# Block-diagonal products moved from GpSimd to VectorE, two small outputs kept as columns, and a new order, in a decode step with its gradients

## The chip, the cores and the metric

One core of a Trainium2 chip runs the kernel. The metric is the device time of one execution in microseconds (us). Before the change the median of seven runs is 478.31 us (475.49 to 484.51).

## The reference

The forward function adds three terms, for a batch of 2 with one position and width D = 576:

```python
xn = _layernorm(x)
out = x + A(xn, k_cache, v_cache, wq, wo) + B(xn, w_gate, w_up, w_down)
# A: q = xn @ wq, 32 heads of 128 on 16 key/value heads, 4096 cached positions
#    p = softmax(q k^T / sqrt(128)); o = p v; o @ wo
# B: (xn @ w_gate * (xn @ w_up)) @ w_down, inner width 4608
```

The kernel returns `out` (out_0) and the gradients for `grad_out` with respect to x (out_1), k_cache and v_cache (out_2, out_3, 2 x 16 x 4096 x 128 each), wq, wo, w_gate, w_up and w_down (out_4 to out_8), all bf16. For each cached head the gradient is a product of a column over positions and a row over the 128 channels: for v it is p times the row of the gradient arriving at o, for k it is the gradient of the scores times q. Two query heads share one cached head, so each such gradient is a sum of two.

## The kernel before, in words

All of k_cache and v_cache is read once (64 tiles of 1 MB) and gradients of the same size are written (64 stores of 1 MB); the weights and their gradients are the rest. Sixteen SBUF buffers of 1 MB, the tiles "big", serve as loaded caches (kv), transposed tiles (X) and outgoing results (st).

Attention goes in 16 steps: step s has a group g of two cached heads (4 query heads) and one batch row b, and in each step k (t = 0) and v (t = 1) are handled for both heads l. Of a step:

- `load_kv` loads the four tiles over SP's DMA queue.
- `turn` transposes each tile in 32x32 blocks on VectorE (L421), in two halves, into an X tile.
- `build_W` copies the query (or the arriving gradient) on GpSimd (POOL) into a stationary operand (L1071).
- `softmax` and `dscore` multiply X by it on TensorE (PE, L1106) and go through chains of small steps that pass between PE, VectorE (DVE) and ScalarE (ACT): L1172 to L1199 and L1227 to L1238. They end in transposed weights pp and dd.
- `build_BD` makes the block-diagonal operand of the outer products. A row of 128 channels per partition (vr) is multiplied by a mask of 16 columns (mask16), so that a tile BD of 128 x 16 x 128 has the row in one block and zeros in the others: L1094, one instruction on POOL for each of 32 cases (16 steps, two for each). There are three BD tiles and two vr tiles.
- `head_outer` multiplies pp or dd by BD on PE (L1128), four units of [128, 2, 512] for each cached head. Each is copied from PSUM into an st tile by ACT (L425) or DVE (L427), and the finished tile goes out on SP (L652).
- `contract` multiplies the weights by the loaded tile (L1283) and folds the result (L1300) into oT; only then is the loaded tile free.

Around these steps run `group_front` and `group_back` (projections with wq and wo and their gradients) and `mlp`, nine slices of the second branch. Their outgoing tiles leave over POOL's DMA queue (L652 as well), and most weights come in over it (L1010 to L1032).

The order is written out while the program is built. Each part is a generator that yields what it needs next: an engine and an estimated cost, a buffer, an event or a DMA. A planner (`Order`) runs these against a clock of its own. It takes the request that can start first; among requests on the same engine within SLACK of that one it takes the lowest priority. `pr(name, s)` is 28 s + PR[name], with HEAD and TAIL added in the first two and the last two steps. An eviction (`EV`) goes to ACT or DVE, whichever would end first. CAP limits how many of the 16 big buffers each use may hold, and LM is a margin that is added to a planned landing. The result is one fixed, in-order list of instructions for each engine and DMA queue. An instruction that waits holds everything behind it on the same engine.

Two small results are summed over the whole kernel. `acc` (128 partitions x 5 x 2, fp32) collects out_0 as columns, and `accx` (128 x 160) collects the gradient of xn. At the end, `final_out` adds x to acc and brings the columns into two rows of 576: L1332 multiplies the saved rows `xy` by an identity, L1346 and L1349 multiply acc by an fp32 identity, L1326 (ACT) and L1327 (DVE) copy the rows, and L1328 stores them on SP. `final_dx` folds accx (L1366, L1368), forms the gradient through the layer norm with DVE steps (L1372 to L1383) and a product with a mean column (L1377), and brings the columns into rows through L1332, L1387 and L1390. At the start, `front` computes the layer norm and also turns x into columns (xnT, L599 to L611).

Of the kernel before, what the change touches and what calls it, by code (L numbers as in the profile page):

```python
# [9 lines left out]
ALU = mybir.AluOpType  # L10
# [3 lines left out]
P = 128  # L14
# [229 lines left out]
def PE(stream, issue=0.0, quad=None, kind="f"):  # L244
    return ("op", "PE", max(CLK * stream, issue) + 0.03, quad, stream, issue, kind)


def DVE(cost):
    return ("op", "DVE", cost)
# [38 lines left out]
def DMA(engine, cost, nbytes, row=8192):  # L288
# [3 lines left out]


NBIG, NGU, NWW, NBD = 16, 1, 5, 3
CAP = {"kv": 8, "X": 8, "st": 12}
MLP0, MLPD = 0, 7.51
KVSTORE = "SP"
WQ0, WO0 = 0, 1
LATENCY, DRY = {"SP": 0.5, "ACT": 0.5, "POOL": 0.57}, 0.4
LM = 0.0  # L300
CLK = 2.0
BIAS = 0.47
SLACK = {"PE": 0.07, "ACT": 0.08, "DVE": 0.41, "POOL": 10.49, "SP": 43.83}
STEP = 28.0
HEAD = {"turn0": 6.6, "att": -11.1, "dsc": 103.3, "con": 16.6, "conv": -58.3, "out1": 57.1, "out0": -106.0, "front": 0.1, "back": -143.5, "W0": 3.2, "W1": 21.7, "BD1": -106.8, "BD0": -0.2, "load": 33.1}
TAIL = {"turn0": 19.4, "turn1": -1.3, "att": 13.2, "dsc": -10.2, "con": -0.3, "conv": -0.3, "out0": 63.9, "front": -9.4, "W0": 5.3, "W1": 19.3, "BD0": -29.4, "load": -20.4}
PR = {"turn0": 125.0, "turn1": -93.7, "att": -589.3, "dsc": -604.4, "conv": 187.4, "con": -216.4, "out1": 1081.4, "out0": 424.1,
      "front": 268.7, "back": 51.9, "W0": 161.4, "W1": 725.8, "BD1": 945.4, "BD0": -58.5, "mlp": -97.3, "wout": -241.3,
      "store": 861.0, "load": 135.3, "wload": -180.4, "fin": 113.9, "const": 215.4, "mload": 362.2}


def pr(name, s):
# [5 lines left out]
def kernel(  # L318
# [128 lines left out]
    meanc = filled("meanc", [P, 1], FP32, 1.0 / D)  # L447
    xnT = filled("xnT", [P, 12], FP32, 0.0)
    nrT = const.tile([P, 4], FP32, name="nrT")
    gg = const.tile([P, 2, 12], FP32, name="gg")  # L450
    gp4 = const.tile([P, 4], FP32, name="gp4")
    zero1 = filled("zero1", [P, 1], FP32, 0.0)
    acc = filled("acc", [P, 5, 2], FP32, 0.0)
# [69 lines left out]
    def carve(t, n):  # L523
        return pairs(t[:])[0:2, D * n:D * (n + 1)]

    xy = const.tile([2, 2 * D], BF16, name="xy")

    def front():
        xb, yb = xy[:, 0:D], xy[:, D:2 * D]
        for t, src in ((xb, A_x), (yb, grad_out)):  # L530
            yield DMA("ACT", 0.45, 2304, 1152)
            nc.scalar.dma_start(t, src.rearrange("b s d -> (b s) d"))
# [55 lines left out]
        yield WAIT(Econst)  # L588
        nr = gg[0:2, 0, 0:4]
        yield DVE(0.3)  # L590
        nc.vector.memset(gg[:, 1], 0.0)
        nc.vector.tensor_scalar(nr[:, 0:2], identf[0:2, 0:2], nmu[:], None, op0=ALU.mult)
        nc.vector.tensor_scalar(nr[:, 2:4], identf[0:2, 0:2], rstd[:], None, op0=ALU.mult)
        i = yield ACQ("m")
        tp, bp = m_t[i], m_t[i][:, 64:68]
        yield PE(0.0, 0.3)
        for a in range(4):
            for c in range(4):
                nc.tensor.matmul(tp[32 * c:32 * c + 32, 2 * a:2 * a + 2], lhsT=xb[:, P * c + 32 * a:P * c + 32 * a + 32],  # L599
                                 rhs=ident[0:2, 0:2], start=True, stop=True)  # L600
        for a in range(2):
            nc.tensor.matmul(tp[0:32, 8 + 2 * a:10 + 2 * a], lhsT=xb[:, 512 + 32 * a:544 + 32 * a],
                             rhs=ident[0:2, 0:2], start=True, stop=True)
        nc.tensor.matmul(bp, lhsT=view(ones[:], 0, 2, 0, [[0, P]]), rhs=nr, start=True, stop=True)
        yield DVE(0.9)
        nc.vector.tensor_copy(xnT[:, 0:8], tp[:, 0:8])
        nc.vector.tensor_copy(xnT[0:32, 8:12], tp[0:32, 8:12])
        nc.vector.tensor_copy(nrT[:], bp)
        for k, op in ((0, ALU.add), (2, ALU.mult)):
            nc.vector.tensor_tensor(xnT[:], xnT[:], view(nrT[:], 0, P, k, [[0, 6], [1, 2]]), op)  # L610
# [465 lines left out]
    def build_BD():  # L1076
        for s in range(NS):
            g, b = divmod(s, Bq)
            for t in (1, 0):
                yield PRIO(pr(f"BD{t}", s))  # L1080
                yield WAIT(Econst)
                yield WAIT(grp[g]["Eq"], grp[g]["Ed"])
                v = yield ACQ("vr")
                m = yield ACQ("m")
                yield PE(0.053)
                nc.tensor.matmul(m_t[m][:, 0:P],
                                 lhsT=qr_t[grp[g]["qs"]][:, t, b, :],
                                 rhs=ident[:], start=True, stop=True)
                e = yield EV(128)
                cp(e, vr_t[v][:], m_t[m][:, 0:P])  # L1090
                yield REL("m", m)
                i = yield ACQ("BD")
                yield POOL(3.6)
                nc.gpsimd.tensor_tensor(BD_t[i][:], view(vr_t[v][:], 0, P, 0, [[0, 16], [1, Dh]]),  # L1094
                                        view(mask16[:], 0, P, 0, [[1, 16], [0, Dh]]), ALU.mult)
                yield REL("vr", v)
                bS[s][t] = i
                yield SET(bE[s][t])
# [223 lines left out]
            yield PRIO(pr("front", 2 * g))  # L1322
            yield from group_front(g)

    def rows_put(o, n, out):
        nc.scalar.copy(view(xy[:], 0, 2, n * D, [[P, 5], [1, 64]]), o[0:2, 0, 0:320].rearrange("p (k n) -> p k n", k=5))  # L1326
        nc.vector.tensor_copy(view(xy[:], 0, 2, n * D + 64, [[P, 4], [1, 64]]), o[0:2, 1, 0:256].rearrange("p (k n) -> p k n", k=4))  # L1327
        nc.sync.dma_start(out.rearrange("b s d -> (b s) d"), xy[:, n * D:(n + 1) * D])  # L1328

    def rows_add(o, n):  # L1330
        for k in range(2):
            nc.tensor.matmul(o[0:2, k, 0:320 - 64 * k], lhsT=ident[0:2, 0:2],  # L1332
                             rhs=view(xy[:], 0, 2, n * D + 64 * k, [[P, 5 - k], [1, 64]]), start=True, stop=False)

    def final_out():
        yield PRIO(PR["fin"])
        yield WAIT(Eprep, *acc_E)
        i = yield ACQ("o")
        o = o_t[i]
        yield PE(1.1, 0.5)  # L1340
        rows_add(o, 0)
        for dc in range(5):
            r = slice(0, P) if dc < 4 else slice(64, P)
            for k in range(2):
                if dc < 4:
                    nc.tensor.matmul(o[0:2, k, 64 * dc:64 * dc + 64], lhsT=acc[:, dc, :],  # L1346
                                     rhs=identf[:, 64 * k:64 * k + 64], start=False, stop=(dc == 3 and k == 1))
            if dc == 4:
                nc.tensor.matmul(o[0:2, 0, 256:320], lhsT=acc[64:P, 4, :], rhs=identf[64:P, 64:P],  # L1349
                                 start=False, stop=True)  # L1350
        yield ACT(0.4)
        yield DVE(0.4)
        yield DMA("SP", 0.3, 2304, 1152)
        rows_put(o, 0, out_0)
        yield REL("o", i)

    def final_dx():
        yield PRIO(PR["fin"])
        yield WAIT(Eprep, *accx_E)
        i = yield ACQ("o")  # L1360
        o = o_t[i]
        m = yield ACQ("m")
        mt = m_t[m]
        g, gx = gg[:, 0], gg[:, 1]
        yield PE(0.3, 0.3)
        nc.tensor.matmul(mt[:, 0:8], lhsT=accx[:, 0:P], rhs=F8[:], start=True, stop=True)  # L1366
        for k in range(2):
            nc.tensor.matmul(mt[0:32, 8:12], lhsT=accx[:, P:160], rhs=F8[:, 4 * k:4 * k + 4],  # L1368
                             start=(k == 0), stop=(k == 1))
        rows_add(o, 1)  # L1370
        yield DVE(0.5)
        nc.vector.tensor_copy(g[:, 0:8], mt[:, 0:8])  # L1372
        nc.vector.tensor_copy(g[0:32, 8:12], mt[0:32, 8:12])
        nc.vector.tensor_tensor(gx, g, xnT[:], ALU.mult)
        nc.vector.reduce_sum(gp4[:], view(gg[:], 0, P, 0, [[12, 2], [1, 2], [2, 6]]), axis=AX.X)
        yield PE(0.0, 0.1)
        nc.tensor.matmul(mt[:, 16:20], lhsT=view(meanc[:], 0, P, 0, [[0, P]]), rhs=gp4[:], start=True, stop=True)  # L1377
        yield DVE(0.5)
        mean = [view(mt[:], 0, P, 16 + 2 * k, [[0, 6], [1, 2]]) for k in range(2)]
        nc.vector.tensor_tensor(gx, xnT[:], mean[1], ALU.mult)  # L1380
        nc.vector.tensor_tensor(gx, g, gx, ALU.subtract)  # L1381
        nc.vector.tensor_tensor(gx, gx, mean[0], ALU.subtract)  # L1382
        nc.vector.tensor_tensor(gx, gx, view(nrT[:], 0, P, 2, [[0, 6], [1, 2]]), ALU.mult)  # L1383
        yield REL("m", m)
        yield PE(0.4, 0.3)
        for a in range(4):
            nc.tensor.matmul(view(o[:], 0, 2, 512 * (a // 2) + 32 * (a % 2), [[64, 4], [1, 32]]),  # L1387
                             lhsT=gx[:, 2 * a:2 * a + 2], rhs=identf[:], start=False, stop=(a == 3))
        for a in range(2):
            nc.tensor.matmul(o[0:2, 0, 256 + 32 * a:288 + 32 * a], lhsT=gx[0:32, 8 + 2 * a:10 + 2 * a],  # L1390
                             rhs=identf[0:32, 0:32], start=False, stop=(a == 1))
        yield ACT(0.4)
        yield DVE(0.4)
        yield DMA("SP", 0.3, 2304, 1152)
        rows_put(o, 1, out_1)
        yield REL("o", i)

    od.spawn(front(), -1000.0)
    od.spawn(final_out(), PR["fin"])
# [42 lines left out]
```

## Time and profile before

| | before |
|---|---|
| median of 7 runs | 478.31 us |
| profiled execution, its own time | 479.3 us |
| its span, first to last instruction | 477.5 us |
| bytes moved | 185.93 MB, mean 389 GB/s |
| ACT evictions of 128x1024 (L425) | 267, mean 1027 ns |
| DVE evictions of 128x1024 (L427) | 41, mean 1212 ns |
| DVE transposes of 128x1024 (L421) of loaded tiles | 128, mean 1217 ns |
| granted TensorE clock, mean | 0.676 |

Engine rows of the profile give the line, the engine, the operation, what is written and read, the count, the busy time and the mean of one; behind the last bar stands the idle time of the engine in front of these instructions, and which instruction ended it. In a timeline the first two figures are the start in us from the span's start and the length. The page cuts the span into 40 slices of some 12 us: a digit is the busy share of a slice in tenths. The DMA share of a window is the mean busy share of the 16 DMA engines; it can read slightly over 1. A DMA engine counts as busy while a packet is under way, so the bytes per second stand beside it.

### The profile page before, as it was taken

How to read it: one execution, taken by the hardware profiler on the slowest of the kernel's cores; microseconds unless marked ns; L12 is line 12 of the kernel's file. 1: busy time of each engine (PE TensorE's matmuls, PEld its weight loads, DVE VectorE, ACT ScalarE, POOL GpSimd, SP SyncE). 2: the span in 40 equal slices, each digit the busy share in tenths (PEclk: the TensorE clock that was granted, in tenths of full speed). 3: DMA queues.
4: the chain of work that ended last, by engine and by line, in shares of the span. 5: the costliest groups of instructions: out<-in, count | busy, mean ns of one | idle time of the engine just before them, and what ended most of it. 6: DMA issues, size and time to landing. Idle time of an engine off the chain costs nothing. (4 is left out here: it accounts for less than half of the span.)

```text
span 477.5 us, 14608 instructions
## 1 busy us (share of the span) xinstructions
PE 374.6 (78%) x6122; PEld 212.2 (44%) x6122; DVE 349.9 (73%) x660; ACT 345.5 (72%) x527; POOL 244.8 (51%) x348
## 2 busy tenths in 40 slices
PE   0589978897869678785987899784989599779886
PEld 0446444444534345433453545433545254424543
DVE  7788777868659567785789856694576799678872
ACT  6069876775886667756787888771878577979984
POOL 6185716647379315593617384673434772664211
PEclk9998685757765666656597855556566675855885
DMA  8999999999999999999999999999999999999985
GB/s 304 386 405 372 410 388 414 406 400 401 419 412 363 390 424 345 379 417 402 419 371 419 410 418 408 402 425 404 410 328 408 421 404 385 405 405 426 360 318 191
DMA packets 33444, 185.93 MB, mean 389 GB/s; under 512 B 5034, under 2 KB 5170, under 8 KB 16994
## 3 DMA queue, kind: packets, MB, share of 16 engines
q1 hardware_dynamic: 19866, 139.61, 72.5%
q0 software_dynamic: 13504, 45.38, 25.3%
q8 instruction: 48, 0.79, 0.6%
q14 instruction: 18, 0.15, 0.1%
q10 hardware_dynamic: 8, 0.00, 0.0%
HBM read 92.48 MB, written 92.48 MB: 387 GB/s over the span
## 5 line engine op out<-in xcount | busy, mean ns | idle before, releaser
L425 ACT CAST big<-ps_o 128x1024 bf16<-128x1024 f32 (+1 forms) x324 | 288.3, 959 | 42.2 <-PE ps_o L1128 27.0
L421 DVE STREAM_TRANSPOSE big<-big 128x1024 f32<-128x1024 f32 x128 | 152.8, 1217 | 11.5 <-issue 4.7
L1094 POOL TENSOR_TENSOR BD<-vr,mask 128x2048 bf16<-128x2048 bf16 x32 | 115.2, 3602 | 43.8 <-ACT vr L425 25.9
L1106 PE MATMUL ps_m<-big,W 128*32 128x128 bf16 x2048 | 61.1, 286 | 10.1 <-DVE big L421 4.4
L427 DVE CAST big<-ps_o 128x1024 bf16<-128x1024 f32 (+1 forms) x52 | 57.8, 1115 | 9.1 <-ACT big L425 4.8
L1106 PEld LDWEIGHTS <-W 128*32 128x32 bf16 x2048 | 48.4, 127 | 29.3 <-issue 28.1
L1128 PE MATMUL ps_o<-BD,pp 32*128 32x512 bf16 x256 | 51.2, 548 | 10.6 <-ACT big L425 5.6
L652 POOL DMA_DIRECT2D out_dram<-big x43 | 33.5, 780 | 38.6 <-ACT big L425 22.1
L1128 PE MATMUL ps_o<-BD,dd 32*128 32x512 bf16 x256 | 47.4, 503 | 7.5 <-ACT big L425 6.1
L1071 POOL COPY W<-rep 32x16 bf16<-32x16 bf16 x128 | 24.8, 194 | 44.0 <-DVE rep L873 39.2
L623 POOL COPY wt<-wm 64x128 bf16<-64x128 bf16 (+1 forms) x34 | 8.9, 263 | 54.7 <-DVE wm L617 51.4
L421 DVE STREAM_TRANSPOSE big<-ww 128x1152 f32<-128x1152 f32 x25 | 34.0, 1360 | 0.3 <-PE ps_m L635 0.3
L1283 PE MATMUL ps_m<-big,dd 128*32 128x512 bf16 x256 | 28.6, 542 | 3.7 <-DVE dd L421 3.2
L1283 PE MATMUL ps_m<-big,pp 128*32 128x512 bf16 x256 | 31.0, 590 | 0.7 <-DVE oT L1303 0.3
L421 DVE STREAM_TRANSPOSE big<-gu 128x1024 f32<-128x1024 f32 x18 | 21.7, 1224 | 6.5 <-DMA out_dram<-big 2.6
L1128 PEld LDWEIGHTS <-pp 32*128 32x128 bf16 x256 | 10.5, 98 | 31.8 <-issue 24.7
L1128 PEld LDWEIGHTS <-dd 32*128 32x128 bf16 x256 | 10.5, 98 | 25.8 <-issue 19.5
L856 PE MATMUL ps_m<-xs,ww 128*128 128x2 bf16 x160 | 5.4, 165 | 17.7 <-DMA ww<-in_A_wq_dram 14.3
L672 PEld LDWEIGHTS <-xnr 32*128 32x128 bf16 x416 | 15.4, 119 | 8.3 <-issue 7.2
L672 PE MATMUL ps_o<-hb,xnr 32*128 32x128 bf16 x288 | 16.1, 277 | 2.4 <-ACT big L425 1.5
L1293 ACT ACTIVATE osb<-ps_m 128x512 bf16<-128x512 f32 x15 | 9.1, 605 | 11.9 <-PE ps_m L1283 11.6
L900 POOL COPY qr<-qd 128x256 bf16<-128x256 bf16 x8 | 3.2, 395 | 28.2 <-ACT qd L898 28.2
(208 smaller groups left out, 581.4 us busy)
## 6 DMA issues: line engine op xcount, KB each, us to landing
out_dram<-big SPq DMA_DIRECT2D x64, 1024.0 KB, 13.9
big<-in_A_k_cache_dram SPq DMA_DIRECT2D x32, 1024.0 KB, 15.1
big<-in_A_v_cache_dram SPq DMA_DIRECT2D x32, 1024.0 KB, 20.0
out_dram<-big POOLq DMA_DIRECT2D x26, 512.0 KB, 11.7
out_dram<-big POOLq DMA_DIRECT2D x17, 576.0 KB, 9.5
ww<-in_B_w_down_dram SPq DMA_DIRECT2D x9, 576.0 KB, 19.0
ww<-in_A_wo_dram POOLq DMA_DIRECT2D x8, 576.0 KB, 15.9
gu<-in_B_w_gate_dram POOLq DMA_DIRECT2D x9, 512.0 KB, 11.8
```

What stands on the lines that cost most here:

```text
L421: nc.vector.transpose(out, in_)
L425: nc.scalar.copy(out, in_)
L427: nc.vector.tensor_copy(out=out, in_=in_)
L623: nc.gpsimd.tensor_copy(view(Wt[:], 64 * h, 64, 0, [[dims[-1][1], n], [1, dims[-1][1]]]), view(Wm[:], 64 * h, 64, off, dims))
L652: (nc.gpsimd if engine == "POOL" else nc.sync).dma_start(dst, src)
L672: nc.tensor.matmul(o[:, aa, dc * P:(dc + 1) * P], lhsT=xnr[32 * a:32 * a + 32, dc * P:(dc + 1) * P], rhs=rhs(a), start=True, stop=True)
L1071: nc.gpsimd.tensor_copy(view(W_t[t][w][:], 32 * a, 32, 6 + 8 * a, [[G * WW, 4], [WW, G], [1, 2]]), view(rep_t[grp[g]["qs"]][:], 32 * a, 32 ...
L1094: nc.gpsimd.tensor_tensor(BD_t[i][:], view(vr_t[v][:], 0, P, 0, [[0, 16], [1, Dh]]), view(mask16[:], 0, P, 0, [[1, 16], [0, Dh]]), ALU.mult)
L1106: nc.tensor.matmul(sc[32 * cq:32 * cq + 32, :], lhsT=view(W[:], 0, P, (be * G + l) * WW + 6 - 4 * c2 - 2 * l, [[1, 32]]), rhs=view(X[:], 0 ...
L1128: nc.tensor.matmul(o[:, k, :], lhsT=pr2[32 * c4:32 * c4 + 32, :], rhs=BD[32 * c4:32 * c4 + 32, 8 * l + 4 * h2:8 * l + 4 * h2 + 4, :], star ...
L1283: nc.tensor.matmul(ct[32 * j:32 * j + 32, :], lhsT=view(rT, 0, P, 4 * c + 2 * l, [[1, 32]]), rhs=kv_t[kvS[s][t][l]][:, Dh * c:Dh * (c + 4) ...
L1293: nc.scalar.activation(ob, cs, AF.Copy, scale=SCALE)
```

## The change

Three things change together. First, `build_BD` gives its product to VectorE, and the planner counts 2.29 us for it in place of 3.6 on POOL:

```diff
-                yield POOL(3.6)
-                nc.gpsimd.tensor_tensor(BD_t[i][:], view(vr_t[v][:], 0, P, 0, [[0, 16], [1, Dh]]),
+                yield DVE(2.29)
+                nc.vector.tensor_tensor(BD_t[i][:], view(vr_t[v][:], 0, P, 0, [[0, 16], [1, Dh]]),
                                         view(mask16[:], 0, P, 0, [[1, 16], [0, Dh]]), ALU.mult)
```

Second, the small results stay columns to the end. `front` turns grad_out into columns as well (goT) and adds the columns of x to acc at once, with 23 more small products on PE and some small steps on DVE. At the end one fp32 transpose gives 10 or 12 rows of 128, one DVE step copies them, and three DMAs on SP store them: one for the first 512 columns of each batch row, and one for the last 64 columns of both.

```diff
-        for a in range(4):
-            for c in range(4):
-                nc.tensor.matmul(tp[32 * c:32 * c + 32, 2 * a:2 * a + 2], lhsT=xb[:, P * c + 32 * a:P * c + 32 * a + 32],
+        for n, row in ((0, xb), (16, yb)):
+            for a in range(4):
+                for c in range(4):
+                    nc.tensor.matmul(tp[32 * c:32 * c + 32, n + 2 * a:n + 2 * a + 2],
+                                     lhsT=row[:, P * c + 32 * a:P * c + 32 * a + 32],
...
+        for dc in range(5):
+            nc.tensor.matmul(tp[:, 32 + 2 * dc:34 + 2 * dc], lhsT=xb[:, DOFF[dc]:DOFF[dc] + P],
                              rhs=ident[0:2, 0:2], start=True, stop=True)
...
+        nc.vector.tensor_copy(goT[:, 0:8], tp[:, 16:24])
+        nc.vector.tensor_copy(goT[0:32, 8:12], tp[0:32, 24:28])
+        nc.vector.tensor_add(acc[:], acc[:], tp[:, 32:42].rearrange("p (k b) -> p k b", b=2))
...
+    def put_row(n, o, out):
+        yield DVE(0.2)
+        row = xy[:, P * n:P * n + P]
+        m = 10 if n == 0 else 12
+        nc.vector.tensor_copy(row[0:m, :], o)
+        for b in range(2):
+            yield DMA("SP", 0.3, 1024, 256)
+            if n == 0:
+                nc.sync.dma_start(out[b, :, 0:512].rearrange("s (k n) -> (s k) n", n=P), row[b:8:2, :])
...
     def final_out():
         yield PRIO(PR["fin"])
         yield WAIT(Eprep, *acc_E)
-        i = yield ACQ("o")
...
+        m = yield ACQ("m")
+        o = m_t[m][0:10, 0:P]
+        yield PE(0.1, 0.1)
+        nc.tensor.transpose(o, acc[:].rearrange("p k b -> p (k b)"), identf[:])
+        yield from put_row(0, o, out_0)
+        yield REL("m", m)
```

`final_dx` does likewise: its last scaling goes into the first DVE steps, grad_out is added as columns, so that three chained DVE steps follow the mean product where four did, and one transpose takes the place of L1332, L1387 and L1390.

Third, the planner's constants are replaced, so that the whole list of instructions stands in another order:

```diff
-CAP = {"kv": 8, "X": 8, "st": 12}
-MLP0, MLPD = 0, 7.51
+CAP = {"kv": 8, "X": 3, "st": 8}
+MLP0, MLPD = 0, 7.79
...
-LM = 0.0
+LM = 2.25
...
-BIAS = 0.47
-SLACK = {"PE": 0.07, "ACT": 0.08, "DVE": 0.41, "POOL": 10.49, "SP": 43.83}
+BIAS = 0.45
+SLACK = {"PE": 0.06, "ACT": 0.12, "DVE": 0.54, "POOL": 13.03, "SP": 44.23}
```

All entries of HEAD, TAIL and PR get other values too, some of them by over 100 (wload -180.4 to 7.8, W1 725.8 to -112.4, wout -241.3 to -466.7).

## The prediction

> **What bounds the kernel now.** I read the page's busy shares and slices first, then the DMA queues, then the windows of the ramp and the tail, then the tail's timeline.
>
> ```profile
> PE 374.6 (78%) x6122; PEld 212.2 (44%) x6122; DVE 349.9 (73%) x660; ACT 345.5 (72%) x527; POOL 244.8 (51%) x348
> DMA  8999999999999999999999999999999999999985
> GB/s 304 386 405 372 410 388 414 406 400 401 419 412 363 390 424 345 379 417 402 419 371 419 410 418 408 402 425 404 410 328 408 421 404 385 405 405 426 360 318 191
> q1 hardware_dynamic: 19866, 139.61, 72.5%
> q0 software_dynamic: 13504, 45.38, 25.3%
> ```
>
> No compute engine is full. The two data queues together fill 72.5 + 25.3 = 97.8% of the 16 DMA engines' span, so the transfers bound it: 185.93 MB in 477.5 us. The page's last slices, 360, 318 and 191 GB/s, say where the time is lost: the end. The bytes stay the same to within some hundred, so time can only be won where the DMA engines go short of work, or lost by making them do so. The windows show this (columns: window, its length, busy us of PE, PEld, DVE, ACT and POOL with their counts, clock, DMA share, GB/s):
>
> ```profile
> 24.00:48.00 24.00, 21.62 (x334) 13.48 (x335) 20.11 (x35) 19.08 (x34) 17.33 (x20) 0.94 1.00 388
> 448.00:466.00 18.00, 15.86 (x296) 9.20 (x292) 13.44 (x25) 14.73 (x21) 4.34 (x9) 0.78 0.79 306
> 466.00:477.50 11.50, 6.97 (x66) 3.90 (x62) 2.40 (x11) 5.43 (x8) 2.11 (x3) 0.50 0.52 196
> ```
>
> Until 448 the queues are nearly full. From 448 to the end 306 x 18 + 196 x 11.5 = 7.76 MB move in 29.5 us; at the 430 GB/s that the 2 us window from 440 shows they would need 18.0. So 11.5 us of the span are a tail in which stores wait for compute. The timeline of the tail (start, length, engine, line) names part of it:
>
> ```profile
> 462.84 0.63 PE L1332 MATMUL ps_o<-xy,ident 2*2 2x320 bf16 x2
> 463.40 1.87 PE L1346 MATMUL ps_o<-identf,acc 128*2 128x64 f32 x16
> 465.20 0.37 PE L1349 MATMUL ps_o<-identf,acc 64*2 64x64 f32 x2
> 465.96 1.55 ACT L425 CAST big<-ps_o 128x576 bf16<-128x576 f32 x2 [2.04 <-PE ps_o L686]
> 472.27 1.87 PE L1387 MATMUL ps_o<-identf,gg 128*2 128x128 f32 x8 [0.87 <-DVE gg L1383]
> 472.35 0.35 SPq L652 DMA_DIRECT2D out_dram<-big  x1
> 474.07 0.37 PE L1390 MATMUL ps_o<-identf,gg 32*2 32x32 f32 x4
> 474.92 0.26 SPq L1328 DMA_DIRECT2D out_dram<-xy  x1
> ```
>
> The row form of the first small output takes PE from 462.84 to about 465.5, in front of the L686 products; ACT stands idle 2.04 us for them, and from 466 to 468 the DMA engines move 4 GB/s. Its twin stands in the last chain.
>
> **The change, part by part. Small results in columns.** For out_0 the row of L1332, L1346 and L1349 (0.63 + 1.87 + 0.37 = 2.87 us) becomes one fp32 transpose. The nearest row, L1180 in the tail, takes 0.27 for a moving 128x128 fp32; with a wait I take 0.35. So 2.5 us come off PE ahead of L686, hence off the last stores. For out_1, L1332's second pair (0.63, from 468.94) stood ahead of the last head's products: off too. Together 3.1 us for the last big store, which issued at 472.35: 469.2. Behind it the chain of out_1 loses L1387 and L1390 (2.24, now 0.35), one of four chained VectorE steps (0.2), and the ScalarE copy (0.41): its DMA, at 474.92, comes some 5.5 earlier less two more issues on SP (three for one, 0.26 each, so 0.5). Both orders of these small DMAs on SP delay a big store by 0.5 at most. The end is then set by the last big store, not by out_1: I count 3.1 less 0.3 for what SP issues ahead of it, 2.8, and 0.5 for the shorter wait for the out_0 bank (PE stood 0.60 for ACT at 467.87). Sum 3.3. If the end stayed with another store, the gain would be nothing; if all cover followed, 5.
>
> **What the front part gains.** 23 more tiny products and, on VectorE, one memset and three or four copies of 0.13 each, at about 18 to 20 us. VectorE stands 0.77 idle at 20.00 for L1106, which hides 0.5 to 0.7; uncovered it would cost 0.7. I take nothing.
>
> **Block-diagonal products.** POOL loses 32 x 3.60 = 115.2 us (245 to 130). VectorE gains 32 products of 2048 columns. No row shows it; the nearest two-input form and the eviction give the slope:
>
> ```profile
> L1094 POOL TENSOR_TENSOR BD<-vr,mask 128x2048 bf16<-128x2048 bf16 x32 | 115.2, 3602 | 43.8 <-ACT vr L425 25.9 <-DVE vr L427 7.6 <-PE ps_m L1180 4.6
> L617 DVE TENSOR_TENSOR wm<-ps_m,mask 128x256 bf16<-128x256 f32 x9 | 3.6, 405 | 0.9 <-PE ps_m L1086 0.3 <-POOL W L1071 0.3 <-PE ps_m L796 0.3
> L427 DVE CAST big<-ps_o 128x1024 bf16<-128x1024 f32 x41 | 49.5, 1212 | 4.2 <-PE ps_o L1128 2.5 <-ACT big L425 1.3 <-issue 0.3
> ```
>
> L617 takes 281 ns at 128 columns and 405 at 256, so 0.97 a column and 2.14 us at 2048; L427's 1212 at 1024 against 754 at 576 gives 1.02 a column and 2.26. I take 2.2. The Trainium skill, "VectorE: DVE Perf Modes", section "The perf-mode tier table", would halve it: 1224 ns for a bf16 product of 2048 in SBUF. But its section "What auto-detection actually checks" asks a step of one in every tensor, and the mask is read with a step of zero in its inner dim; so the slow form stands. By one price 32 x 2.2 = 70.4 us on VectorE, by the other 39. VectorE goes from 349.9 to 420, and with ScalarE, which shares the evictions, from 695.4 to 766 of 2 x 477.5 = 955, 80%. On the average that fits, and the transfers hide it.
>
> A rule that speaks against the move: "SBUF — State Buffer", section "Who interferes with whom", says that VectorE and GpSimd share one port pair under an exclusive lock, which a VectorE step with two SBUF inputs also takes. The trace shows such a stall at the start, where small VectorE steps last as long as POOL's memsets beside them:
>
> ```profile
> 3.72 2.53 DVE L501 CAST mask<-mk 128x16 bf16<-128x16 f32 x1
> 4.75 0.63 POOL L483 MEMSET wm<- 128x280 bf16 x2
> ```
>
> In the steady part POOL's copies (L1071, L623, L900) are 36.9 us, 8% of the time, so 32 products meet two or three of them at under 0.9 us each: 2 us in all on VectorE, hidden. Without the rule: 0. The other way, POOL's copies wait up to 2.2 us behind a product, where they waited up to 3.6 in POOL's own line; POOL's 122 DMA issues no longer stand behind a product at all. I give that nothing either: the waits show POOL waiting for others, not the reverse.
>
> Where the cover is thin is the ramp. From 28 to 44 us VectorE is busy 3.56 + 3.89 + 3.59 + 3.81 = 14.9 of 16 and ScalarE 13.7; POOL does two products there and its third starts at 26.68. Three on VectorE, 6.6 us, make 35.2 of 32: 3.2 us too many, in a stage where the DMA share already dips (0.92 from 36 to 40). Behind a queued product stand the 1.2 us transposes, and the scores wait for those. Against it, a product is there 1.4 us sooner (2.2 for 3.6), and PE waited for the first at 30.34. Cost between -0.4 and 3.2; I take 1.0.
>
> **The order.** All priorities change; X tiles go from 8 to 3 and stores from 12 to 8 of the 16 big buffers, and loads are planned to land 2.25 us later. Do the caps bind? X serves 64 + 18 + 16 = 98 tiles: three allow 3 x 477.5 / 98 = 14.6 us each, against two transposes of 1.2 and the score. Big stores number 64 + 43 = 107: eight allow 35.7 us each, of which 14 or less is the landing. So the caps leave room. The later landings take stalls from the in-order engines (PE waits 14.3 us for wq at L856 and 6.3 for w_up), none of which the transfers feel until the tail. The tail keeps 11.5 - 3.3 = 8.2 us of shortage, and the dips before it about 2: the most an order could win is 10. It can lose as much as the rival below. Taken: 2.0 won, a fifth of what is there, as the tail's work is short of neither VectorE (13.4 of 18) nor ScalarE (14.7 of 18).
>
> Sum on the profiled execution's own time: 479.3 - 3.3 + 0 + 1.0 - 2.0 = 475.0. That run lies 1.0 over the median of 478.31, so 474.0.
>
> **The rivals.** Slower: VectorE's in-order queue becomes the bound wherever two products fall into one full 12 us window. Two cost 4.4, so windows with VectorE and ScalarE over 19.6 of 24 overflow: 36 to 48 (21.8) by 2.2, 48 to 60 by 0.3, 84 to 96 by 0.1, 240 to 252 by 0.5, 384 to 396 (20.5) by 0.9, 396 to 408 by 0.2, 432 to 444 (22.9) by 3.3, 444 to 456 (21.3) by 1.7: 9.2 us. With the 3.3 won it is 485.2, 484 as a median. For it speak the full ramp and tail; against it that the queues hold 14 to 20 us of transfers ahead (the landings), so only starving longer than that shows. It decides once the starving passes the 3.3.
>
> No change: out_0 and out_1 get short, but another late store takes the end, and the ramp gives back the rest: 477.5 to 479, say 478.3. For it: 472.35 for the last big store lies only 2.6 before the last small one. The change also might not do what it says at the end: small stores of 256-byte rows, three each, could land later than one of 1152; with 0.5 for two issues each this stays in the same case.
>
> **How the numbers follow.** Likeliest, 0.53: 474.0, its own range 467 to 475.9. No change, 0.15: 478.3. Slower, 0.32: 484, from 480.7 to 491. What a measurement here can tell from no change is about 0.5%, 475.9 to 480.7. The range takes the likeliest's low side and most of the rival: 467 to 487.
>
> **What would show it.** Right: L1094 rows on VectorE at 2.2 us; the tail without L1346 and L1387, the last big store at about 469 of a span of 473 to 474; 24 to 48 us with a DMA share of 0.97 or more. Wrong: DMA shares under 0.95 in slices before the last three, VectorE over 90% with idle time on ScalarE, or a tail in which stores still come late after 466; a product at 1.2 us would make the ramp's 1.0 too much.

## The result, and the profile after

The changed kernel takes 484.46 us (median of 12 runs) against 477.85 us (31 runs): ratio 1.014, 95% interval 1.0113 to 1.0166. It is slower by 6.6 us, where about 4 less was forecast. Ratios, here and below, are taken from fast runs, those within 1.5% of the fastest of their kernel, so they can differ a little from the ratio of the medians. Its profiled execution took 482.4 us with a span of 480.7. This pair of profiles (482.4 and 479.3) shows 3.1 of the 6.6, since the one lies 2.0 under its median and the other 1.4 over its own. The page after, in the order of the lines shown of before:

```profile
PE 372.3 (77%) x6113; PEld 212.6 (44%) x6113; DVE 403.3 (84%) x683; ACT 356.3 (74%) x538; POOL 132.5 (28%) x316
DMA  8997999999999999999999999999999999999977
GB/s 303 386 375 282 372 410 419 370 380 412 406 389 329 406 423 371 378 413 421 398 413 400 411 424 371 371 410 408 419 417 384 410 423 408 399 389 421 394 280 277
q1 hardware_dynamic: 19924, 139.61, 72.8%
q0 software_dynamic: 13504, 45.38, 24.8%
```

The bytes are the same and the two queues are still full on the whole (97.6%). New is the fourth slice: 282 GB/s where 372 stood, and a 7 in the DMA row. Added up over 12 us windows, the changed kernel is 0.40 MB behind the kernel before at 36 us, 1.91 at 60 and 2.93 at 156, stays 1.9 to 3.2 behind until 444, and makes it up only in the tail. At some 410 GB/s the 1.91 MB are 4.7 us. The three windows of before, after the change:

```profile
24.00:48.00 24.00, 16.60 (x255) 9.45 (x255) 19.27 (x28) 12.94 (x25) 5.00 (x13) 0.62 0.88 329
448.00:466.00 18.00, 14.82 (x268) 8.15 (x267) 15.66 (x29) 16.63 (x25) 3.90 (x7) 0.81 0.79 313
466.00:480.70 14.70, 7.04 (x90) 4.21 (x88) 5.93 (x18) 6.76 (x9) 2.55 (x5) 0.52 0.77 298
```

In the ramp the share is 0.88 and ScalarE is busy for 12.9 of 24 us (19.1 before): it has nothing to evict. The last stretch moves 298 GB/s where it moved 196: the tail is better, as forecast. The timeline of the ramp, changed kernel:

```profile
31.41 2.27 DVE L1104 TENSOR_TENSOR BD<-vr,mask 128x2048 bf16<-128x2048 bf16 x1
36.92 1.38 DVE L421 STREAM_TRANSPOSE big<-ww 128x1152 f32<-128x1152 f32 x1 [3.03 <-DMA ww<-in_B_w_down_dram]
38.22 0.12 DVE L1245 TENSOR_TENSOR cr<-ps_m,rz 128x1 f32<-128x1 f32 x1
42.30 0.35 SPq L662 DMA_DIRECT2D out_dram<-big  x1
```

The first product starts at 31.41 on VectorE (26.68 on POOL before). Then VectorE stands 3.03 us in front of a weight that lands at 36.9, with dscore's small steps behind it. The first 1 MB store issues at 42.30; before, two had been issued from 34.77 on. The product and the tail's steps:

```profile
L1104 DVE TENSOR_TENSOR BD<-vr,mask 128x2048 bf16<-128x2048 bf16 x32 | 72.5, 2265 | 0.3 <-ACT vr L425 0.2
```

```profile
468.09 0.38 PE L1359 MATMUL ps_m<-identf,acc 128*10 128x128 f32 x1
...
473.42 0.36 SPq L662 DMA_DIRECT2D out_dram<-big  x1
...
475.15 0.38 PE L1389 MATMUL ps_m<-identf,gg 128*12 128x128 f32 x1 [0.67 <-DVE gg L1386]
...
475.87 1.85 SPq L1345 DMA_DIRECT2D out_dram<-xy  x2
477.78 0.65 SPq L1351 DMA_DIRECT2D out_dram<-xy  x1
```

A product costs 2265 ns, so the slow form holds (2.2 taken), and none of the 32 lasts longer than 2315. POOL is the one that waits where both meet:

```profile
288.12 2.58 POOL L633 COPY wt<-wm 64x128 bf16<-64x128 bf16 x2 [21.29 <-DVE wm L627]
288.24 2.31 DVE L1104 TENSOR_TENSOR BD<-vr,mask 128x2048 bf16<-128x2048 bf16 x1
```

One of these two copies lasts 2242 ns, where the median of the line is 282. It happens to two copies of the changed kernel, and to none of the kernel before, where the longest of this line takes 304. So the shared port that the prediction names costs POOL some 4 us in all, and VectorE nothing that shows.

A transpose of 0.38 stands in for 2.87 us of PE. From the first product on accx to the first small store of out_1 it is now 3.6 us (472.26 to 475.87) where it was 6.8 (468.11 to 474.92), but SP then takes 2.5 us for three small stores; one took 0.26.

### The profile page after: what moved, and what is told of

It reads as the page before. It is cut to its first block, busy times and chain, and to the rows that moved or that the text cites. A ratio compares the mean times of both kernels' runs of the same rounds, so it can differ in the third digit from the quotient of the medians.

```text
span 480.7 us, 14549 instructions
## 1 busy us (share of the span) xinstructions
PE 372.3 (77%) x6113; PEld 212.6 (44%) x6113; DVE 403.3 (84%) x683; ACT 356.3 (74%) x538; POOL 132.5 (28%) x316
## 4 chain that ended last, share of the span: by engine, by line
DMA 20%; PE 17%; ACT 12%; DVE 9%; issue 4%; SPq 0%; DVEq 0%; ACTq 0%
DMA out_dram<-big 20%; ACT big L425 10%; DVE big L421 4%; PE ps_o L1138 4%; PE ps_m L1116 4%; PE ps_m L1293 3%; DVE big L427 2%; PE ps_o L682 1%; DVE BD L1104 1%; PE ps_m L899 1%; PE ps_m L640 1%; PE ps_m L1123 0%; PE ps_m L1204 0%; PE ps_m L1243 0%; PE ps_o L731 0%
## 5 line engine op out<-in xcount | busy, mean ns | idle before, releaser
L425 ACT CAST big<-ps_o 128x1024 bf16<-128x1024 f32 (+1 forms) x336 | 299.9, 966 | 47.2 <-PE ps_o L1138 36.3
L1104 DVE TENSOR_TENSOR BD<-vr,mask 128x2048 bf16<-128x2048 bf16 x32 | 72.5, 2265 | 0.3 <-ACT vr L425 0.2
L1116 PE MATMUL ps_m<-big,W 128*32 128x128 bf16 x2048 | 58.5, 279 | 6.4 <-DVE oT L1313 1.7
L427 DVE CAST big<-ps_o 128x1024 bf16<-128x1024 f32 (+1 forms) x40 | 43.7, 1093 | 4.3 <-PE ps_o L1138 2.7
L633 POOL COPY wt<-wm 64x128 bf16<-64x128 bf16 (+1 forms) x34 | 12.7, 375 | 92.4 <-DVE wm L627 89.1
L1293 PE MATMUL ps_m<-big,dd 128*32 128x512 bf16 x256 | 27.1, 516 | 0.7 <-DVE dd L421 0.4
L425 ACT CAST sp<-ps_m 128x256 bf16<-128x256 f32 x26 | 10.0, 386 | 13.8 <-PE ps_m L1124 13.6
L776 PE MATMUL ps_m<-big,Wdy 128*128 128x128 bf16 x162 | 16.4, 280 | 4.4 <-DVE cr L1245 3.1
L776 PEld LDWEIGHTS <-Wdy 128*128 128x128 bf16 x162 | 14.7, 129 | 6.7 <-issue 4.2
```

The source lines that it names most:

```text
L425: nc.scalar.copy(out, in_)
L427: nc.vector.tensor_copy(out=out, in_=in_)
L633: nc.gpsimd.tensor_copy(view(Wt[:], 64 * h, 64, 0, [[dims[-1][1], n], [1, dims[-1][1]]]), view(Wm[:], 64 * h, 64, off, dims))
L776: nc.tensor.matmul(dh, lhsT=Wdy[:, e, 2 * k:2 * k + P], rhs=view(X[:], 0, P, 64 * k + e, [[D, FC], [2, 32]]), start=(k == 0 and e == 0), s ...
L1104: nc.vector.tensor_tensor(BD_t[i][:], view(vr_t[v][:], 0, P, 0, [[0, 16], [1, Dh]]), view(mask16[:], 0, P, 0, [[1, 16], [0, Dh]]), ALU.mult)
L1116: nc.tensor.matmul(sc[32 * cq:32 * cq + 32, :], lhsT=view(W[:], 0, P, (be * G + l) * WW + 6 - 4 * c2 - 2 * l, [[1, 32]]), rhs=view(X[:], 0 ...
```

## Experiments

All times are compared with the kernel before on the same chips; its medians there are 478.5 to 479.7. Three theories run through the expectations: (1) the products stand in VectorE's line while the ramp (here the first 60 us) is full; (2) their load on VectorE bounds the middle; (3) the new order is the cause and the products are not. "Same order" means that the planner counts what it counted, so each engine gets the list it had except for what the edit moves.

**One part of the change at a time, first four.** Columns alone, on the kernel before. Front and end are edited as in the change's diff, but the planned costs of the front are those of before, so that the list stays the same outside front and end (this cut is against the changed kernel):

```diff
-        yield PE(0.0, 0.6)
+        yield PE(0.0, 0.3)
...
-        yield DVE(1.3)
+        yield DVE(0.9)
```

> The kernel before with the columns alone: products on POOL, constants and order of before, only the front's extra steps and the column form of the end. The prediction's step says -3.3 from 477.9, so 474.6. With SP's issues at 2.2 us for each output instead of 0.26, the gain on PE and in the chain stays but 2 us of it are given back: 476 to 477.

476.2 us, ratio 0.996 (0.9936 to 0.9985): a gain of 1.9 us, and the interval lies below 1. So this part is good, and smaller than the 3.3 taken. The timeline of its end, in which the last big store issues 6.35 us earlier than the 472.35 of before (this profiled span is 4.0 shorter):

```profile
459.76 0.38 PE L1359 MATMUL ps_m<-identf,acc 128*10 128x128 f32 x1
...
466.00 0.36 SPq L662 DMA_DIRECT2D out_dram<-big  x1
...
467.62 1.81 SPq L1345 DMA_DIRECT2D out_dram<-xy  x2
469.47 0.65 SPq L1351 DMA_DIRECT2D out_dram<-xy  x1
```

Not all of the 6.35 is the columns' doing: at 444 us this profile is already 0.77 MB ahead of that of before, with the same list, which is 1.9 us at 410 GB/s. And the store is on its way for 6.5 us where it was 3.9, so it lands only 3.7 us earlier.

The products back on POOL in the changed kernel, same order:

```diff
                 yield DVE(2.29)
-                nc.vector.tensor_tensor(BD_t[i][:], view(vr_t[v][:], 0, P, 0, [[0, 16], [1, Dh]]),
+                nc.gpsimd.tensor_tensor(BD_t[i][:], view(vr_t[v][:], 0, P, 0, [[0, 16], [1, Dh]]),
```

> The changed kernel with all 32 block-diagonal products back on POOL, every other instruction in the same order on its engine. If the ramp is lost because the first products stand in VectorE's line (theory 1), the first outer product comes before 32 us, the DMA share of 36 to 48 us rises from 0.74 to over 0.9, and the time falls from 484.5 by 2 to 5, to 480 to 482. If VectorE's 73 us more are the bound through the middle (theory 2), it falls by 5 or more, to 479 or less. If the order is the cause and the products are not (theory 3), it stays within 1.5 of 484.5 or gets worse, as products of 3.6 come late in an order that counts on 2.29.

493.3 us, ratio 1.0324 (1.0277 to 1.0372): worse, as theory 3 allowed. The new order needs its products fast; this run doesn't say yet that they cost nothing.

The first w_down on another queue, changed kernel, same order:

```diff
-            nc.sync.dma_start(ww_t[d][:, 0:FC * D].rearrange("p (c n) -> p c n", c=FC),
+            (nc.sync if i else nc.scalar).dma_start(ww_t[d][:, 0:FC * D].rearrange("p (c n) -> p c n", c=FC),
```

> The changed kernel with only the first load of w_down issued on ScalarE's DMA queue instead of SP's, where it stands behind eight loads of 1 MB. In the changed kernel it lands at 36.9 us, VectorE waits 3.0 us for it with the chain of dscore and the second product behind. If that landing is what empties the DMA queues (theory 1b), the wait is gone, the share of 36 to 48 us rises from 0.74 to 0.85 or more and the time falls by 2 to 3.5, to 481 to 482.5. If the products in VectorE's line are the cause (1) or the load of the middle (2), it changes by under 1.

485.2 us, ratio 1.013 (1.0072 to 1.0187): no change that the interval shows. (In a_wdown_first below, which has the same edit, VectorE starts on that weight at 33.91 us without a wait.) Taking away the 3.03 us wait that the ramp shows so plainly wins nothing that can be seen by itself.

The small stores on three queues, changed kernel, same order (out_1's two lines likewise):

```diff
-                nc.sync.dma_start(out[b, :, 0:512].rearrange("s (k n) -> (s k) n", n=P), row[b:8:2, :])
+                (nc.scalar if b else nc.sync).dma_start(out[b, :, 0:512].rearrange("s (k n) -> (s k) n", n=P), row[b:8:2, :])
...
-            nc.sync.dma_start(out[:, 0, 512:576], row[8:10, 64:P])
+            nc.gpsimd.dma_start(out[:, 0, 512:576], row[8:10, 64:P])
```

> The changed kernel with the six small stores at the end spread over three queues: the second batch row on ScalarE's, the last 64 columns on POOL's. SP's issues of them took 1.78 + 0.43 and 1.85 + 0.65 us in the changed kernel where the row form took 0.26 each. If the span ends by this issuing, the last store is issued 1.5 us earlier and the time falls by 1 to 2, to 482.5 to 483.5; if the landing of the last big store sets the end, it stays within 0.5 of 484.5.

486.1 us, ratio 1.0177 (1.0121 to 1.0232): no gain. The issuing on SP is not the end. From 480 to 482 us 339 GB/s still move, 3 to 5 us after the last big store issued at 477.02; the small ones had all issued by 480.3. That big store lands 6.0 us after its issue, at 483. In the changed kernel it is 5.9 and in the kernel before 3.9, and there the span ends 1.3 us after that landing. When the small stores on SP land, the traces don't show.

**Where the products run and which constants plan them.** The kernel before with its products on VectorE, POOL's 3.6 still planned:

```diff
                 yield POOL(3.6)
-                nc.gpsimd.tensor_tensor(BD_t[i][:], view(vr_t[v][:], 0, P, 0, [[0, 16], [1, Dh]]),
+                nc.vector.tensor_tensor(BD_t[i][:], view(vr_t[v][:], 0, P, 0, [[0, 16], [1, Dh]]),
```

> The kernel before with only the 32 products on VectorE, in the order of before, which did not plan for them. If VectorE's load is a bound through the middle (theory 2), the time rises by 5 or more, to 483 or over, with a DMA share under 0.97 in several windows between 60 and 440 us. If only the ramp is thin (theory 1), the DMA engines lose 1 to 4 us before 60 us and nothing lasting behind: 479 to 482. If neither, within 1 of 477.9.

508.2 us, ratio 1.0625 (1.058 to 1.0671). This is more than any rival said. Two windows of it, and the chain between them:

```profile
336.00:348.00 12.00, 5.27 (x108) 2.85 (x108) 11.36 (x14) 2.62 (x4) 0.00 (x0) 0.64 1.02 425
348.00:360.00 12.00, 11.18 (x166) 7.58 (x168) 8.00 (x22) 8.83 (x16) 3.82 (x13) 0.50 0.69 275
```

```profile
335.69 2.25 DVE L1094 TENSOR_TENSOR BD<-vr,mask 128x2048 bf16<-128x2048 bf16 x1
338.45 0.27 PE L1113 MATMUL ps_m<-ds,identP 128*128 128x128 bf16 x1 [2.60 <-DVE ds L1238]
341.74 0.27 ACT L425 CAST vr<-ps_m 128x128 bf16<-128x128 f32 x1 [3.98 <-PE ps_m L1086]
348.35 0.30 ACT L1184 COPY mr<-m 1x128 f32<-1x128 f32 x1 [5.05 <-DVE m L1182]
```

In the first, VectorE is busy 11.36 of 12 us, two products among its 14 instructions, while ScalarE works 2.62 and PE 5.27. In the next the DMA share is 0.69. The load adds up to well under both engines' time, but it stands in one line, and the work of the others waits behind it: the small steps of dscore (L1235, L1238) start when the product ends at 337.9, PE waits 2.60 us for them, and ScalarE 3.98 for PE and then 5.05 for VectorE again.

The constants of the change alone, on the kernel before (products planned at 3.6 on POOL, rows; every constant from CAP to PR, of which two are shown):

```diff
-CAP = {"kv": 8, "X": 8, "st": 12}
+CAP = {"kv": 8, "X": 3, "st": 8}
...
-LM = 0.0
+LM = 2.25
```

> The kernel before with only the new planner constants (caps, priorities, margin), products on POOL and the row form of the end, planned again with POOL's 3.6. If the order is the cause (theory 3), 482 to 486 and VectorE waits for the first w_down at about 34 to 37 us. If the products on VectorE are (1 and 2), within 2 of 477.9.

484.9 us, ratio 1.013 (1.0078 to 1.0181): the order alone, with every product on POOL, costs 6.2 us. The ramp was kept here: its bytes at 60 us equal those of before. The loss lies at 240 to 264 (309 and 364 GB/s, where before moved 373 and 422) and in the tail (193 GB/s at 444 to 456, where before moved 328). So theory 3's number came without the wait that its expectation named.

The constants of before on the changed kernel, that is the same block the other way round:

> The changed kernel with the planner constants of before: products on VectorE at a planned 2.29 us, columns, the old caps and priorities, planned again. If the new constants are the cause (theory 3), 475 to 478. If the products on VectorE are (1 and 2), 481 to 486, with the DMA share of 36 to 48 us under 0.9.

517.2 us, ratio 1.0816 (1.0773 to 1.0859): 33 us more than with the new ones. Neither set of constants serves the other kernel. The ramp falls 1.42 MB short at 60 us here too. So its shortage comes with the move of the products and the list planned for it, and not with the new constants.

Both mends of the ramp together, changed kernel (w_down on ScalarE's queue, the two products of step 0 on POOL):

> The changed kernel with the first w_down load on ScalarE's queue and the first two products (step 0) on POOL, all else in the same order. If the ramp is the whole loss, the cumulated bytes at 60 us come within 0.5 MB of the kernel before (1.9 MB short in the changed kernel), and the time falls by 4 to 5, to 479.5 to 480.5. If the two mends don't add, 481 to 482.

487.2 us, ratio 1.0185 (1.0143 to 1.0227). The deficit at 60 us is 1.80 MB against 1.91: nothing mended. The first store came 2.9 us earlier (39.41), but wq now issued behind the product on POOL, and PE waited 2.71 us for it at 41.69. One wait took the place of the other.

**What the products cost, by leaving them out.** Only the first use of each of the three BD tiles is built, the other 29 products are gone, on either kernel, same order:

```diff
-                nc.vector.tensor_tensor(BD_t[i][:], view(vr_t[v][:], 0, P, 0, [[0, 16], [1, Dh]]),
-                                        view(mask16[:], 0, P, 0, [[1, 16], [0, Dh]]), ALU.mult)
+                if 2 * s + 1 - t < 3:
+                    nc.vector.tensor_tensor(BD_t[i][:], view(vr_t[v][:], 0, P, 0, [[0, 16], [1, Dh]]),
+                                           view(mask16[:], 0, P, 0, [[1, 16], [0, Dh]]), ALU.mult)
```

> The changed kernel with 29 of its 32 products left out (BD tiles stale, so out_2 and out_3 are not the gradients), same order. If VectorE's 66 us of products are what costs (theory 2), the time falls from 484.5 to 478 or less, DMA shares over 0.97 in the middle. If the new order has its own shortage in the ramp (three products remain there) and around 144 to 156 us (theory 3), it stays at 482 to 486.

484.8 us, ratio 1.014 (1.0091 to 1.0189): the same as with all 32, to within some 2 us. VectorE falls from 403.3 to 342.8 us busy and the time doesn't move:

```profile
PE 373.8 (78%) x6113; PEld 214.7 (45%) x6113; DVE 342.8 (71%) x654; ACT 355.3 (74%) x538; POOL 129.2 (27%) x316
```

```profile
24.00:48.00 24.00, 18.17 (x263) 10.83 (x263) 19.81 (x27) 13.52 (x24) 5.13 (x14) 1.00 0.93 342
144.00:156.00 12.00, 11.61 (x168) 5.06 (x167) 7.65 (x12) 11.42 (x16) 6.13 (x15) 0.50 0.94 302
```

The second of these windows in the kernel before:

```profile
144.00:156.00 12.00, 10.55 (x172) 5.33 (x171) 11.60 (x18) 7.79 (x12) 11.32 (x13) 0.57 1.00 358
```

The ramp is short here too (342 GB/s, 1.63 MB behind at 60 us), at a granted clock of 1.00 where the changed kernel's profile had 0.62, so the clock doesn't explain it. The products are not cleared for the ramp: the three that are left stand there, and the first that is gone would have started at 61 us. With them on POOL the ramp stays short as well (1.69 MB in a_bd_pool, 1.80 in a_wdown_first), but there each takes 3.6 us in a list that counts on 2.29. From 61 us on the case is clear: without any product the same list takes the same time. At 144 to 156 VectorE has 4 us to spare and still 302 GB/s move. That shortage belongs to the list.

> The kernel before with 29 of its 32 block-diagonal products left out (each BD tile is built once and read stale later, so out_2 and out_3 are not the gradients), same order. It bounds what freeing POOL of the products can win. If the products on POOL hold nothing up, as the prediction's zero says, within 1 of 478.5. If POOL's queue of DMA issues or the outer products waited for them, 473 to 476.

475.2 us, ratio 0.9954 (0.9929 to 0.9979). Even if they cost nothing elsewhere, freeing POOL of 29 products is worth 2.2 us in the list of before.

**The ramp against the rest**, on the kernel before, same order: only step 0's two products on VectorE, then only the other 30.

```diff
-                nc.gpsimd.tensor_tensor(BD_t[i][:], view(vr_t[v][:], 0, P, 0, [[0, 16], [1, Dh]]),
+                (nc.vector if s == 0 else nc.gpsimd).tensor_tensor(BD_t[i][:], view(vr_t[v][:], 0, P, 0, [[0, 16], [1, Dh]]),
```

> The kernel before with only the first two products (step 0) on VectorE, all else in the order of before. If the full ramp alone turns 4.5 us of products into a lasting loss (theory 1), the bytes at 60 us fall 0.8 to 1.9 MB short and the time rises by 2 to 4.5, to 481 to 483. If the ramp has room, within 1 of 478.5.

478.5 us, ratio 0.9983 (0.996 to 1.0006): no loss. The bytes do fall behind, by 1.14 MB at 72 us and still 1.30 at 336, but 0.8 MB of it comes back between 336 and 360, where the profile of before has a dip:

```profile
36.00:48.00 12.00, 9.01 (x142) 5.52 (x131) 11.51 (x21) 9.86 (x15) 3.60 (x1) 1.00 0.86 329
348.00:360.00 12.00, 9.25 (x179) 5.17 (x176) 7.96 (x11) 7.78 (x10) 3.51 (x6) 0.67 1.01 381
```

Before moved 370 in the first window and 334 in the second. The dip itself is not firm: b_columns and b_columns_spread have the same list there and move 406 and 350 in the second window, and 333 and 364 in the first. Half a MB in one profile is thus within what one list shows. What holds is the time: a delay of some 2.8 us in the transfers at 72 us left nothing at the end.

> The kernel before with the other 30 products on VectorE and the first two on POOL, same order. All 32 gave 508. If losses in the middle and tail make up most of it (theory 2), 500 to 506, with the bytes at 60 us within 0.5 MB of before. If the ramp is the source of what comes later, under 490.

505.7 us, ratio 1.0557 (1.0511 to 1.0602): nearly all of the 508.2 comes from the other 30, with losses from step to step (1.5 MB at 48 us, 3.7 at 216, 8.7 at 432). The expectation's bound for 60 us failed, since step 1's products lie in the ramp as well.

**How much a plan is worth.** The planned cost of one product changed by 20 to 100 ns, nothing else; the kinds and durations of the instructions stay, their order differs (and the odd eviction changes its engine). The first edit, and then 3.55 and 3.7 likewise, and 2.27 and 2.32 for the 2.29 of the changed kernel:

```diff
-                yield POOL(3.6)
+                yield POOL(3.65)
```

> The kernel before planned with 3.65 us for a product on POOL in place of 3.6, nothing else. If its order is one among many alike, within 1.5 of 478.5. If its constants fit that one plan only, the list comes out otherwise and the time rises by 3 or more, to 481 to 490, with the instructions and their durations unchanged; then each experiment that plans anew carries such a loss.

3.65 on POOL: 487.4 us, ratio 1.0205 (1.0158 to 1.0251).

> The kernel before planned with 3.55 for a product on POOL instead of 3.6. With 3.65 it took 487.4. If the order of before is a selected one among plans of 482 to 490, this gives 482 to 490 too, and loses in another place than the tail from 432 us on. If 3.65 was an outlier, within 1.5 of 478.5.

3.55 on POOL: 502.0 us, ratio 1.0468 (1.0419 to 1.0517).

> The kernel before planned with 3.7 for a product on POOL instead of 3.6, a third draw: 482 to 490 if the order of before is a selected one; within 1.5 of 478.5 if not.

3.7 on POOL: 501.5 us, ratio 1.0428 (1.0375 to 1.0481).

> The changed kernel planned with 2.27 for a product (it measures 2.265) instead of 2.29, nothing else. If its constants fit one plan only, as those of before do (3.65 for 3.6 gave 2% more), 488 to 496. If a plan with products on VectorE is simply slow by its load and all such plans are alike, 483 to 486. Under 479 would mean that the changed kernel's own order is a bad draw.

2.27 on VectorE: 501.8 us, ratio 1.0475 (1.0426 to 1.0523).

> The changed kernel planned with 2.32 for a product instead of 2.29. A second draw of its plan: if plans with the products on VectorE scatter above those with POOL (485 and 487 so far), 488 to 500; if both kinds scatter alike, 482 to 490.

2.32 on VectorE: 500.1 us, ratio 1.0425 (1.0385 to 1.0466). These plans of before lie at 487 to 502 and those of the changed kernel at 500 to 502, against 478 and 484.5 for the two lists as they stand. The first plan of before (3.65) keeps pace with the bytes of before to 432 us, up to 1.3 MB ahead, and breaks only in the tail, where before moved 328 and 269 GB/s in these two windows:

```profile
444.00:456.00 12.00, 10.72 (x159) 5.46 (x156) 9.24 (x18) 11.28 (x16) 4.65 (x7) 0.57 0.67 244
456.00:468.00 12.00, 10.45 (x147) 3.81 (x146) 6.68 (x13) 8.95 (x13) 6.29 (x2) 0.71 0.45 184
```

Another (3.55) breaks at 360 to 384 us, at 237 and 266 GB/s. No engine is full in either place: stores stand on SP in a sequence in which the next one isn't ready. Between 432 and 470 us SP stands 31.4 us in front of stores for ScalarE's evictions in the first of these plans, where it is 13.1 before; VectorE's are 8.2, where they were 16.4.

**The best version.** Columns with the small stores spread:

> The kernel before with the columns, and the small stores spread over SP's, ScalarE's and POOL's queues. With the columns alone it took 0.996 of before, 476.2. If SP's issuing of the small stores still sets the end, 1 to 1.5 less, 474.5 to 475.5; if the last big store's landing does, the same within 0.5.

477.1 us, ratio 0.998 (0.9956 to 1.0005): no better than the columns on SP alone. The kernel before with columns, 476.2, is the fastest complete one found; it beats both kernels.

## Why the prediction was wrong

**The bound** was read rightly on the average: the transfers, with the two queues 97.6% full after the change.

**The step that failed** is the order: "the most an order could win is 10. It can lose as much as the rival below. Taken: 2.0 won, a fifth of what is there, as the tail's work is short of neither VectorE (13.4 of 18) nor ScalarE (14.7 of 18)". The new constants alone, on the kernel before, lose 6.2 us (b_order), with the ramp intact: the term was off by about 8 us and had the wrong sign. (That list, too, is one draw from the planner.) The whole change says the same. The columns are worth -0.4% (in the old list; in the new one they were not tried alone), and the products' time from 61 us on nothing (a_none). So of the measured +1.4% about +1.8%, 8.6 us, is left for the new list and its ramp together, where the prediction had -2.0 and +1.0; how much of it is the ramp the runs don't tell. The working looked at what an order could win from free engine time. What the runs show is that the list of before stands out among its neighbours: 50 ns more or less in one planned cost gives 487 or 502. The list of the changed kernel stands out as well, since 20 and 30 ns in its plan give 502 and 500; it comes out above the old one all the same. Free engine time says nothing on this; the plans that break have it too (VectorE 6.68 and ScalarE 8.95 of 12 us at 456 to 468 with 3.65).

**The caps**: that they leave room on the average may be right; no run took them alone, and an average would not have shown a starved place anyway.

**The ramp** was placed rightly and sized wrongly both ways. Its starvation is larger than the 1.0 (4.7 us of bytes at 60 us), and b_first_dve shows that such a loss need not last: 1.14 MB behind at 72 us and no time lost. In the changed kernel the bytes stayed behind. The runs that put step 0's, step 1's or all products on VectorE are 0.95 to 1.9 MB short at 60 us; those on the kernel before that leave them on POOL are at most 0.4. Which instruction of the ramp's list starves it stays open: the two visible waits were taken away together, and another came in.

**The products** were costed rightly (2265 ns against 2.2 us). Of the stalls through the port shared with POOL, the prediction put 2 us on VectorE and up to 2.2 on each copy of POOL that meets a product: the second came (two copies of 2.2 us in the changed kernel, four of 2.1 to 2.5 in b_bd_dve), the first did not. That "the transfers hide it" holds in the list made for it, at least from 61 us on (a_none), and fails by 6% in a list not made for it (b_bd_dve), so where they run and the order are one decision. The zero for POOL's freed queue was some 2.2 us too low (b_none, 1.0 to 3.4), which is what the whole move could have won in the list of before. (POOL's DMA issues were counted as 122; the trace lists 128, which changes nothing here.)

**The columns** gained 1.9 of the 3.3. The PE time and the chain went about as worked out (one transpose of 0.38 us against 0.35 taken); the size of the issue was missed (2.5 us for three small stores, counted as 0.8). Yet spreading them brought nothing, which fits an end that is set by the last big store's landing; and that store takes 6.5 us to land in b_columns and 5.9 in the changed kernel, where it was 3.9 before, a term that the prediction's sum did not have. How much of the missing 1.4 is which, the runs don't tell.

**The rival** that named 484 hit the number by luck. Its mechanism, two products in a full window, shows in b_bd_dve, but not in the changed kernel, where leaving the products out changes nothing. Of the other 3.5 us between the medians, which the first pair of profiles doesn't show, a part may lie at 132 to 156 us: in a_spread, which runs the same list until the end, the two 12 us windows move 359 and 282 GB/s where the first profile of the changed kernel has 388 and 329, 0.9 MB less.

**Open**: whether more choosing would bring a list with the products on VectorE under 476, which constants make the new list short, and what the columns are worth in it.

## What to carry to other kernels

When a change comes with a new static order, ask first how much a plan is worth: change one planned cost by 1% and time it. If that moves the time more than the change is meant to, the gain has to be shown in lists of equal quality, and a part kept in the old order (here the columns) is the safer way to take it. A visible wait in a starved stage is a candidate and not a cause: remove it and count the bytes at the end of the stage and at the end of the kernel.

## What was not expected of the hardware

A small store on SP takes the queue longer than its bytes suggest: 0.26 us for two rows of 1152 bytes, 0.9 us each for the four rows of 128 columns and 0.4 to 0.65 for the 64-column rest. The granted clock of the same list at 24 to 48 us was 0.62 in one profile and 1.00 in another (a_none, without most of its products), with 1.91 and 1.63 MB missing at 60 us: the clock moved little here, where the transfers bound the kernel.
